# Double-buffered v, the first expert's arithmetic on GpSimd and wider slot rows in an attention and mixture-of-experts kernel

## The chip, the cores and the metric

The kernel runs on one core of a Trainium2 chip. The metric is the device time of one launch in microseconds. Three runs of the kernel before took 496.51, 497.23 and 498.8 us; their median is 497.23.

## What is computed

Causal attention over 4 batches of 12 heads (448 positions, 64 dimensions, float32), and then, on its output as 1792 rows of 768, a mixture of eight experts in which each row goes to its best expert only:

```python
scores = scale * np.matmul(q, k.transpose(0, 1, 3, 2))
scores = np.where(mask, -1000000000.0, scores)
attn = np.exp(scores - np.max(scores, axis=-1, keepdims=True))
attn = attn / (np.sum(attn, axis=-1, keepdims=True) + 1e-09)
x = np.matmul(attn, v)                       # 4 x 12 x 448 x 64, then rows of 768
...
logits = x @ w_gate + modality_bias[modality_id]
e_idx = np.argmax(logits, axis=1)
probs = softmax(logits)
out[mask] = gate_w[mask, None] * (np.maximum(x[mask] @ w1[e], 0.0) @ w2[e])   # for each expert e
```

## The kernel before

Float32 products are made from two parts: an operand is split into a high part (rounded to TensorE's fp32r) and a low part (the rest), and the product is three or four passes. The first three pairs of heads, the six that run before the split operands are ready, are multiplied in plain float32. Every split is one `tensor_scalar` (high) and one `tensor_tensor` (low) on some engine, and in attention most of them are GpSimd's.

**Attention** is a software pipeline. `iteration(n)`, n from 0 to 47 (the last heads' later stages follow behind), starts the scores of head n on TensorE (L270, `st_scores`), the exponentials of head n-1 on ScalarE (L290), the transposes (L302) and the split of the probabilities of head n-2 (L320 on ScalarE, L321 on VectorE), the product with v of head n-3 (L334, L341) and its output (L359, L365). Heads go in pairs m for q and k and in groups `gr` of four (`GH`) for v. For each pair GpSimd runs `split_qk` (L194, L195) and `split_kl` (L200 for the low part of k, L202 twice for q with one half zeroed, `qz`); SyncE stacks the parts with DMAs (L211, L212). For each group it runs `split_vh` (L242) and `split_vl` (L247) out of the one buffer `vraw`; those of group g + 1 stand at the end of iteration n = 4g + 2, and the next group's `load_v` (L235, L236), which must wait until they have read the buffer, at the start of n = 4g + 4.

A group's output is multiplied by wi, which holds both the identity and the gate's weights, and so gives rows of x and their partial logits. They are divided by the row sums in `norm_l` (L412) and `norm_x` (L422), on VectorE or, for the last of four row tiles, on GpSimd from a copy by ScalarE (L404). When a batch's last group is through (n = 19, 31, 43 for batches 0 to 2), `after_batch` puts its routing into the lists `later`, `before` and `soon`, which the iterations work off: logits (L454, VectorE), the best expert with ties broken (L457 to L470), slot numbers by a small chain of matmuls (`places`, L476 to L482) and a scatter of row numbers and gate weights into four tables in DRAM (L501, GpSimd's indirect DMA). Batch 3's routing runs after the pipeline. GpSimd also makes the constants (`setup_1`, `setup_4`, `shift_slots`, each a chain of instructions on a few elements) and splits w1 chunks 0, 1, 2, 3 and 5 of the first expert (L675, L676); from batch 1 the kernel already knows the expert with the most rows (`first_expert`, `first_slot`, `first_shift`, L516 to L537, VectorE).

**The end of attention** starts the first expert: `pre_g1(t, ks)` multiplies step t's rows by w1 chunks ks (L751 to L753). In the order of the code: pre_g1(0, 3 and 4), `places` of batch 3, pre_g1(1, 0 to 3), the ranks and batch 3's scatter, pre_g1(0, 5), relu, pre_g1(1, 4), the transposes of step 0, and so on. `ids_for(1)` then reads step 1's slots back from the tables, `fetch_x(1)` gathers its rows (L732, GpSimd) and L741 transposes them. From there to the end the experts' steps run on TensorE almost without a gap.

Every engine works its own queue in program order; so where an instruction stands in GpSimd's queue decides what must be done ahead of it. An entry of a table is 8 bytes; an expert has 1792 places of its own in a table, followed by an empty region, 14592 entries in all.

Of the kernel before, what the change touches and what calls it, by code (L numbers as in the profile page):

```python
# [21 lines left out]
def attention_moe(  # L22
# [23 lines left out]
    GH = 4  # L46
# [14 lines left out]
    NS = 32  # L61
    EMPTY = E * NT
    NROW = EMPTY + 2 * BLK
    BIG = 30000
# [10 lines left out]
    def sm(shape, tag, dt=F32, bufs=2):  # L75
        return small.tile(shape, dt, tag=tag, name=tag, bufs=bufs)
# [148 lines left out]
    def first_load(m):  # L225
        nc.sync.dma_start(out=first_view(m, 2), in_=qk[0, m, :, 1])
        for a in range(2):
            r = slice(a * 64, a * 64 + 64)
            (nc.sync if m or a else nc.scalar).dma_start(out=first_view(m, a)[r], in_=qk[0, m, r, 0])
            spl[2 * m + a] = (first_view(m, a), first_view(m, 2), None, None)  # L230

    def load_v(gr):
        b, u = divmod(gr, NG)
        c = slice(u * GH * D, (u + 1) * GH * D)
        nc.sync.dma_start(out=vraw[:, 0:3, :], in_=v[b, 0:384, c].rearrange("(t p) c -> p t c", p=128))  # L235
        nc.sync.dma_start(out=vraw[0:64, 3, :], in_=v[b, 384:448, c])  # L236

    vsrc = vraw.rearrange("p t (h d) -> p t h d", h=GH)

    def split_vh(gr):  # L240
        t = T([128, NTL, GH, 2, D], F32R, "vhl", 2)
        P.tensor_scalar(out=t[:, :, :, 0], in0=vsrc, scalar1=1.0, scalar2=0.0, op0=ALU.mult, op1=ALU.add)  # L242
# [198 lines left out]
    def route(b):  # L441
# [30 lines left out]
        def places():  # L472
            prev = rt[b - 1][0][:, NP:] if b else ebase
# [12 lines left out]
            A.activation(out=pe[:, :, 0:E], in_=lg, func=AF.Exp)  # L486
            rt[b] = (pc, si)
# [19 lines left out]
        if b == B - 2:  # L507
            choose = ((1, logits), (1, top), (1, ties), (2, first_tie), (-3, choice))
        return choose, places, (slots, ranks), scatter
# [4 lines left out]
    def counts(b):  # L514
        cnt = sm([128, E], "cnt")
        V.tensor_tensor(out=cnt, in0=rt[b][0][:, NP:], in1=ebase, op=ALU.subtract)  # L516
        return cnt
# [3 lines left out]
    def first_expert():  # L521
        cnt = counts(1)
        fe["m"] = m = sm([128, 1], "fm")
        fe["t"] = t = sm([128, E], "ft")
        V.tensor_reduce(out=m, in_=cnt, axis=AX, op=ALU.max)
        V.scalar_tensor_tensor(out=t, in0=cnt, scalar=m, in1=e8[:, 0, :], op0=ALU.is_ge, op1=ALU.mult)

    def first_slot():
        V.tensor_reduce(out=xf, in_=fe["t"], axis=AX, op=ALU.max)
        V.scalar_tensor_tensor(  # L530
            out=sch0[0:1, 0:1 + NPRE], in0=sch_a, scalar=xf[0:1], in1=sch_b, op0=ALU.mult, op1=ALU.add
        )
        V.tensor_scalar(out=oh0, in0=fe["t"], scalar1=xf, scalar2=None, op0=ALU.is_equal)

    def first_shift():
        V.tensor_scalar(out=shift, in0=fe["m"], scalar1=float(2 * BLK), scalar2=None, op0=ALU.is_lt)
        V.scalar_tensor_tensor(out=now, in0=by_shift[1], scalar=shift, in1=by_shift[0], op0=ALU.mult, op1=ALU.add)  # L537

# [29 lines left out]
    def schedule_a(cnt):  # L568
# [13 lines left out]
        def ts(o, a, x, y, op0, op1):  # L582
            V.tensor_scalar(out=o, in0=a, scalar1=x, scalar2=y, op0=op0, op1=op1)
# [41 lines left out]
        red(r, base)  # L625
        ts(sch[:, 0:1], r, float(EMPTY), 0.0, ALU.add, ALU.add)
        return seg, oh
# [81 lines left out]
    def fetch_ids(t, off, blk=0):  # L709
        d = early.tile([128, NTL, 2, 2], I32, tag="idq", name="idq", bufs=3)  # L710
        for i in range(NTL):
            o = d[:, i, blk]
            if t == 0 or PZ <= t < SZ:
                src = tables[i][bass.ds(off, BLK), :]
            elif t < PZ:
                o = d[:, i]
                src = tables[i][bass.ds(off, 2 * BLK), :].rearrange("(b p) c -> p b c", p=BLK)
            else:
                src = tables[i][bass.ds(off, HB), :].rearrange("(o p) c -> o p c", o=1).to_broadcast([2, HB, 2])
            nc.sync.dma_start(out=o, in_=src)  # L720
        idq[t, blk] = d
# [155 lines left out]
    with tc.manual_schedule():  # L877
# [51 lines left out]
        ti = it[:, 256:257]  # L929
        P.memset(onesf, 1.0)  # L930
        P.memset(eq, 0.5)
        P.memset(sch_a, -float(NT))
        P.memset(sch_a[:, 0:1], -1.0)
        for j in range(1 + NPRE):
            P.memset(sch_b[:, j:j + 1], float(E * NT + (j - 1) * BLK) if j else float(E))
        for j in range(2):
# [16 lines left out]
        def later(n, f):  # L953
            todo.setdefault(n, []).append(f)
# [30 lines left out]
        def setup_1():  # L985
            cmp(gpos, eq1, 0.0, ALU.is_gt)
            P.tensor_tensor(out=gt64, in0=gpos, in1=gt64, op=ALU.mult)
            cmp(eq1, eq1, -1.0, ALU.is_equal)
            cmp(ctri, ctri, 0.0, ALU.is_gt)
            fma(e8, evals, -1.0, float(E))  # L990
            P.tensor_copy(e8v, e8)
            fma(ebase, evals[:, 0, :], float(NT), 0.0)
            fma(ebneg, ebase, 1.0, -float(EMPTY))

        later(0, setup_0)
        later(1, setup_1)
        later(2, lambda: V.memset(e8v[64:128, 0], 0.0))

        def setup_4():
            P.iota(ent[:, :, 0, 0], pattern=[[S, B]], base=0, channel_multiplier=1)  # L1000
            P.iota(ent[:, :, 1:NTL, 0], pattern=[[S, B], [128, NTL - 1]], base=64, channel_multiplier=1)
            for i in range(NTL):
                nc.sync.dma_start(out=tables[i].rearrange("(p r) c -> p r c", p=128), in_=fill)
            it = row()
# [25 lines left out]
        def after_batch(b, n):  # L1030
# [4 lines left out]
            for j, f in choose:  # L1035
                later(n + j, f) if j > 0 else before(n - j, f)
            last = b == B - 2
            soon(n + 4, places)
# [35 lines left out]

        for k in range(KA):
            later(NHEAD - KA + k, lambda k=k: w1_chunk(k, P))
        later(4, setup_4)
        for s in range(2):
            for j in range(3):
                later(6 + 3 * s + j, lambda s=s, j=j: shift_slots(s, j))  # L1080

        def iteration(n):
            if n % 2 == 1 and 5 < n + 3 < NHEAD:
                stack_qk((n + 3) // 2)
            if n == 1:
                load_v(1)
            if n and n % GH == 0 and n // GH + 1 < B * NG:
                load_v(n // GH + 1)
            gr, i = divmod(n - 2 * GH, GH)
# [17 lines left out]
            if n == 0:  # L1107
                split_vh(0)
                split_vl(0)
            if n % 2 == 1 and 5 < n + 3 < NHEAD:  # L1110
# [18 lines left out]
            if 0 <= gr < B * NG:  # L1129
                st_comb(gr, i)  # L1130
            if n % GH == 2 and n // GH + 1 < B * NG:
                split_vh(n // GH + 1)
                split_vl(n // GH + 1)
            if n in (1, 3):
                load_qk(4 + n // 2)
            if n % 2 == 0 and n > 3 and n + 8 < NHEAD:
                load_qk((n + 8) // 2)

        for n in range(NHEAD):
# [99 lines left out]
        def w2_chunk(*ks):  # L1239
            split_w(raw20, w2h, w2l, ks)  # L1240
# [185 lines left out]
```

## Time and profile before

| | |
|---|---|
| median of three runs | 497.23 us (496.51 to 498.8) |
| the profiled execution | 498.88 us, its span 496.8 us |
| mean granted TensorE clock | 0.987 |
| TensorE busy (matmul) | 470.7 us, 95% |
| VectorE, ScalarE, GpSimd busy | 290.3, 276.4, 245.8 us |
| DMA | 78.91 MB, mean 159 GB/s |

The table is of one profiled execution; its own time stands beside its span because the span leaves out what lies around the first and last instruction. Shares are means over the span: attention fills about the first 210 us, the experts the rest, and GpSimd, VectorE and ScalarE are much busier in the first part.

### The profile page before, as it was taken

The numbers are of one execution on the slowest core, as the hardware profiler recorded it, in microseconds if no ns is written. First come the engines' busy times: TensorE is split into PE (matmuls) and PEld (weight loads), VectorE is DVE, ScalarE is ACT, GpSimd is POOL, SyncE is SP. The second block draws the span as 40 slices with busy tenths as digits, with TensorE's granted clock in tenths as the row PEclk, the third lists the DMA queues.
The fourth block names the chain that finished last, engine by engine and source line by source line (L and its number), as shares of the span: only waits on it lengthen the run. The fifth ranks groups of instructions, "written<-read, shape, count | busy, mean of one in ns | idle before, by whom it ended". The sixth has DMA issues, their size and how long they took to land. (4 is left out here: it accounts for less than half of the span.)

```text
span 496.8 us, 10248 instructions
## 1 busy us (share of the span) xinstructions
PE 470.7 (95%) x3307; PEld 443.0 (89%) x3307; DVE 290.3 (58%) x858; ACT 276.4 (56%) x680; POOL 245.8 (49%) x332
## 2 busy tenths in 40 slices
PE   8999899999899979989999999999999999999990
PEld 6799899999798979869999999999999999889770
DVE  4899899999889988987422017431120120283490
ACT  5799899999788978326212116612220211383670
POOL 8999999999999999942301104102001001021131
PEclk9999999999899999989999999999999999999997
DMA  7797799998987889491596204853001001076200
GB/s 189 199 257 214 183 236 251 281 237 206 292 214 182 188 182 327 126 202 3 163 381 208 81 1 144 292 203 98 34 1 53 33 2 63 33 279 194 104 13 7
DMA packets 43816, 78.91 MB, mean 159 GB/s; under 512 B 15582, under 2 KB 27614, under 8 KB 43744
## 3 DMA queue, kind: packets, MB, share of 16 engines
q1 hardware_dynamic: 40624, 66.94, 49.2%
q0 software_dynamic: 3040, 11.03, 6.6%
q8 instruction: 28, 0.46, 0.5%
q14 instruction: 44, 0.36, 0.3%
q10 hardware_dynamic: 80, 0.11, 0.1%
HBM read 48.10 MB, written 11.89 MB: 121 GB/s over the span
## 5 line engine op out<-in xcount | busy, mean ns | idle before, releaser
L732 POOL DMA_INDIRECT xg<-xs,idg x18 | 21.0, 1164 | 156.6 <-DVEq L1336 80.8
L290 ACT ACTIVATE p<-p,nm 128x448 f32<-128x448 f32 x192 | 94.8, 498 | 2.5 <-DVE nm L280 2.5
L770 DVE SCALAR_TENSOR_TENSOR htl<-g,hth 128x256 fp32r<-128x256 f32 x40 | 16.7, 425 | 104.6 <-ACT hth L769 104.6
L751 PE MATMUL g<-xh,w1h 128*128 128x256 f32 x240 | 67.1, 280 | 0.4 <-DVE htl L770 0.4
L753 PE MATMUL g<-xh,w1l 128*128 128x256 f32 x240 | 67.3, 280 | 0.0
L752 PE MATMUL g<-xl,w1h 128*128 128x256 f32 x240 | 67.0, 279 | 0.0
L321 DVE TENSOR_TENSOR pl<-pt,ph 128x1024 fp32r<-128x1024 f32 x48 | 58.3, 1215 | 7.6 <-ACT ph L320 7.2
L302 PE MATMUL pt<-ident,p 128*128 128x128 f32 x480 | 60.2, 273 | 0.0
L302 PEld LDWEIGHTS pt<-ident,p 128*128 128x128 f32 x480 | 55.3, 141 | 1.1
L334 PE MATMUL ot<-ph,vhl 128*128 128x448 f32 x192 | 50.5, 303 | 5.9 <-DVE ut L365 5.9
L320 ACT ACTIVATE ph<-pt 128x1024 fp32r<-128x1024 f32 x48 | 49.1, 1023 | 7.4 <-PE pt L302 6.3
L769 ACT ACTIVATE hth<-g 128x256 fp32r<-128x256 f32 x40 | 15.1, 383 | 63.5 <-PE g L753 63.5
L751 PEld LDWEIGHTS g<-xh,w1h 128*128 128x128 f32 x240 | 44.9, 187 | 0.6 <-DVE htl L770 0.6
L811 POOL DMA_INDIRECT out_dram<-row,idg x14 | 16.2, 1157 | 59.1 <-ACTq L1320 33.5
L752 PEld LDWEIGHTS g<-xl,w1h 128*128 128x128 f32 x240 | 45.2, 188 | 0.0
L753 PEld LDWEIGHTS g<-xh,w1l 128*128 128x128 f32 x240 | 45.1, 188 | 0.0
L334 PEld LDWEIGHTS ot<-ph,vhl 128*128 128x128 f32 x192 | 33.2, 192 | 7.9 <-DVE ut L365 6.4
L280 DVE CUSTOM_DVE_ANT_0 p<-sa,mask 128x448 f32<-128x448 f32 x96 | 36.2, 412 | 5.2 <-PE sa L270 4.9
L290 ACT ACTIVATION_READ_ACCUMULATOR p<-p,nm 128x1 f32 x192 | 36.5, 190 | 0.0
L280 DVE CUSTOM_DVE_ANT_0 p<-sb,mask 128x192 f32<-128x192 f32 x96 | 36.3, 411 | 0.0
L341 PE MATMUL ot<-pl,vhl 128*64 128x64 f32 x192 | 35.1, 298 | 0.7 <-DVE pl L321 0.7
L359 ACT ACTIVATE hol<-ot 64x448 f32<-64x448 f32 x48 | 26.0, 542 | 13.3 <-PE ot L334 10.8
(365 smaller groups left out, 1307.6 us busy)
## 6 DMA issues: line engine op xcount, KB each, us to landing
st<-hl SPq DMA_DIRECT2D x56, 224.0 KB
raw<-in_moe_w_dram SPq DMA_DIRECT2D x24, 512.0 KB
raw<-in_qk_dram SPq DMA_DIRECT2D x21, 448.0 KB
raw<-in_moe_w_dram SPq DMA_DIRECT2D x20, 384.0 KB
vraw<-in_v_dram SPq DMA_DIRECT2D x12, 384.0 KB
xs<-row SPq DMA_DIRECT2D x9, 384.0 KB
w1h<-hl SPq DMA_DIRECT2D x14, 224.0 KB
w1l<-hl SPq DMA_DIRECT2D x14, 224.0 KB
```

The source lines that it names most:

```text
L280: V.tensor_tensor_reduce(out=z, in0=o, in1=m, scale=-scale, scalar=3.0e38, op0=ALU.add, op1=ALU.min, accum_out=nm[:n, i:i + 1],)
L290: A.activation(out=z, in_=z, func=AF.Exp, bias=nm[:n, i:i + 1], scale=-1.0, accum_out=sums[:n, b, i, h:h + 1],)
L302: nc.tensor.transpose(out=o, in_=a, identity=i)
L320: A.activation(out=ph, in_=t, func=AF.Copy)
L321: V.tensor_tensor(out=pl, in0=t, in1=ph.bitcast(F32), op=ALU.subtract)
L334: nc.tensor.matmul(o[:, q0:S], lhsT=t[:rows, kt, h].rearrange("p a d -> p (a d)"), rhs=ph[:rows, c0:c1], start=(n == 0), stop=(n == 1),)
L341: nc.tensor.matmul(o[0:D, q0:S], lhsT=t[:rows, kt, h, 0], rhs=pl[:rows, c0:c1], start=False, stop=False)
L359: A.activation(out=t, in_=ov[g][64:128, :S], func=AF.Copy)
L732: P.indirect_dma_start(out=xg[u][:n], out_offset=None, in_=xs[0:rows, :], in_offset=bass.IndirectOffsetOnAxis(ap=g[:n, 0:1], axis=0), boun ...
L751: nc.tensor.matmul(o, lhsT=ah, rhs=bh, start=first, stop=False)
L752: nc.tensor.matmul(o, lhsT=ah, rhs=bl, start=False, stop=False)
L753: nc.tensor.matmul(o, lhsT=al, rhs=bh, start=False, stop=last)
```

## The change

The change has several parts. Places in the text of the kernel after the change have other line numbers (L412 becomes L421, L676 becomes L691, and so on).

- **v has two buffers**: `vraw`, and a raw w1 tile for even groups from 2 on. Loads go out earlier, at n = 1, 4 and then 4g + 2; `split_vh` moves from the end of n = 4g + 2 to that of 4g + 3, and so from ahead of the L412 of that iteration to behind it; `split_vl` goes to the end of n = 4g + 4. The very first `split_vl` goes from GpSimd to VectorE.
- **The first expert's arithmetic** goes from VectorE (six instructions, two reductions stay) to GpSimd (eleven).
- **The constants**: `setup_4` at n = 1 and not 4; the tables are cleared at n = 5; all of `shift_slots` at n = 3 and not over n = 6 to 11; one more constant.
- **Batch 2's choice** of expert stands ahead of the first w1 split.
- **Slot rows** are 64 bytes apart (every eighth 8-byte entry), the tables 20480 entries long; the slot numbers are multiplied by 8 where ScalarE copies them (L485 of the kernel before), and divided again for the counts.
- **The end**: pre_g1(0, 5) stands ahead of `places`; 32 warm-up matmuls in place of 24.

```diff
-    EMPTY = E * NT
-    NROW = EMPTY + 2 * BLK
+    STEP = 8
+    SHIFT = 64
+    EMPTY = STEP * (NT + E * SHIFT)
+    NROW = EMPTY + STEP * 2 * BLK
...
+    vraws = [vraw, raw1[2].rearrange("p (t c) -> p t c", t=NTL)]
+    def v_of(gr):
+        return vraws[gr > 1 and gr % 2 == 0]
...
-    def split_vl(gr):
+    def split_vl(gr, eng):
         t = vhl[gr]
-        P.tensor_tensor(out=t[:, :, :, 1], in0=vsrc, in1=t[:, :, :, 0].bitcast(F32), op=ALU.subtract)
+        eng.tensor_tensor(out=t[:, :, :, 1], in0=vsrc(gr), in1=t[:, :, :, 0].bitcast(F32), op=ALU.subtract)
...
-            A.activation(out=pc, in_=pos[:, 0:NP + E], func=AF.Copy)
+            A.activation(out=pc, in_=pos[:, 0:NP + E], func=AF.Copy, scale=float(STEP))
...
     def first_expert():
-        cnt = counts(1)
+        cnt = sm([128, E], "cnt")
+        ts(cnt, rt[1][0][:, NP:], 1.0 / STEP, 0.0)
+        P.tensor_tensor(out=cnt, in0=cnt, in1=ebase, op=ALU.subtract)
         V.tensor_reduce(out=m, in_=cnt, axis=AX, op=ALU.max)
-        V.scalar_tensor_tensor(out=t, in0=cnt, scalar=m, in1=e8[:, 0, :], op0=ALU.is_ge, op1=ALU.mult)
+        P.tensor_scalar(out=t, in0=cnt, scalar1=m, scalar2=0.0, op0=ALU.is_ge, op1=ALU.add)
+        P.tensor_tensor(out=t, in0=t, in1=e8[:, 0, :], op=ALU.mult)
...
     def first_slot():
         V.tensor_reduce(out=xf, in_=fe["t"], axis=AX, op=ALU.max)
-        V.scalar_tensor_tensor(
-            out=sch0[0:1, 0:1 + NPRE], in0=sch_a, scalar=xf[0:1], in1=sch_b, op0=ALU.mult, op1=ALU.add
-        )
-        V.tensor_scalar(out=oh0, in0=fe["t"], scalar1=xf, scalar2=None, op0=ALU.is_equal)
+        P.tensor_scalar(out=sch_a, in0=sch_a, scalar1=xf[0:1], scalar2=0.0, op0=ALU.mult, op1=ALU.add)
+        P.tensor_tensor(out=sch_a, in0=sch_a, in1=sch_b, op=ALU.add)
+        P.tensor_copy(sch0[0:1, 0:1 + NPRE], sch_a)
+        P.tensor_scalar(out=oh0, in0=fe["t"], scalar1=xf, scalar2=0.0, op0=ALU.is_equal, op1=ALU.add)
...
-                src = tables[i][bass.ds(off, BLK), :]
+                src = tables[i][bass.ds(off, BLK, STEP), :]
...
-        for _ in range(24):
+        for _ in range(32):
...
-            later(3 + j, lambda j=j: V.memset(xg[j], 0.0))
+            later(2 * j, lambda j=j: V.memset(xg[j], 0.0))
...
-        later(2, lambda: V.memset(e8v[64:128, 0], 0.0))
+        later(3, lambda: V.memset(e8v[64:128, 0], 0.0))
...
-        for k in range(KA):
-            later(NHEAD - KA + k, lambda k=k: w1_chunk(k, P))
-        later(4, setup_4)
+        later(1, setup_4)
+        later(5, clear_tables)
         for s in range(2):
             for j in range(3):
-                later(6 + 3 * s + j, lambda s=s, j=j: shift_slots(s, j))
+                later(3, lambda s=s, j=j: shift_slots(s, j))
...
-            if n % GH == 2 and n // GH + 1 < B * NG:
+            if n == 1:
+                split_vl(0, V)
+            if n == 2 or n % GH == 3 and n > GH and n // GH + 1 < B * NG:
                 split_vh(n // GH + 1)
-                split_vl(n // GH + 1)
+            if n == 2 or n % GH == 0 and n > GH:
+                split_vl((n + 2) // GH, P)
...
         pre_g1(0, (3, 4))
+        pre_g1(0, (5,))
         places()
         pre_g1(1, (0, 1, 2, 3))
...
-        pre_g1(0, (5,))
         ha, hb = (relu(o, i) for i, o in enumerate(g1b[0]))
-        w2_chunk(2)
         pre_g1(1, (4,))
         pa, pb = two_banks()
         h_trans(0, ha, 0, pa)
+        w2_chunk(2)
```

GpSimd's queue near the start, before the change: the split of pair 3 (heads 6 and 7) around the v split of group 1, then the first of setup_4's instructions (L1000 on).

```order
L194 TENSOR_SCALAR hl<-raw_121 128x896
L195 TENSOR_TENSOR hl<-raw_121,hl 128x448
L242 TENSOR_SCALAR vhl<-vraw 128x16x64
L247 TENSOR_TENSOR vhl<-vraw,vhl 128x16x64
L200 TENSOR_TENSOR xh<-raw_121,hl 128x448
L202 TENSOR_SCALAR w1h_147<-raw_121,half 128x448 x2
L1000 IOTA ent 128x4
L1001 IOTA ent 128x4x3
```

The same place after the change, from the second of the two slot tables' instructions on (those of the first, and setup_4, stand ahead of this piece; L202 and L204 are L200 and L202 of before):

```order
L559 TENSOR_SCALAR by_shift_99<-tcol 128x1 x2
L559 TENSOR_SCALAR by_shift_99<-by_shift_99 128x1 x2
L559 TENSOR_SCALAR slot<-by_shift_99 128x1
L571 TENSOR_SCALAR by_shift_99<-by_shift_99,slot 128x1
L559 TENSOR_SCALAR slot<-by_shift_99 128x1
L571 TENSOR_SCALAR by_shift_99<-by_shift_99,slot 128x1
L573 TENSOR_TENSOR by_shift_99<-by_shift_99,by_shift_98 128x4
L202 TENSOR_TENSOR xh<-raw_121,hl 128x448
L204 TENSOR_SCALAR w1h_147<-raw_121,half 128x448 x2
```

All 17 instructions of the slot tables and the eight of setup_4 now stand ahead of the last two splits of pair 3; before, they stood behind them.

GpSimd's queue where the first expert is found, iterations 37 and 38, after the change (`cnt`, `ft`, `sch_a` and `oh_95` are the counts, the candidates, the schedule's first row and the one-hot choice; `fm` and `xf` come from VectorE):

```order
L256 TENSOR_TENSOR vhl<-vraw,vhl 128x16x64
L559 TENSOR_SCALAR cnt<-pc 128x8
L537 TENSOR_TENSOR cnt<-cnt,ebase 128x8
L539 TENSOR_SCALAR ft<-cnt,fm 128x8
L540 TENSOR_TENSOR ft<-ft,e_80 128x8
L202 TENSOR_TENSOR xh<-raw_120,hl 128x448
L204 TENSOR_SCALAR qz_155<-raw_120,half 128x448 x2
L381 TENSOR_SCALAR rec<-sums 128x16
L544 TENSOR_SCALAR sch_a<-sch_a,xf 1x3
L545 TENSOR_TENSOR sch_a<-sch_a,sch_b 1x3
L546 CAST sch_110<-sch_a 1x3
L547 TENSOR_SCALAR oh_95<-ft,xf 128x8
```

Before, the splits and L381 (then L372) follow one another there with none of the eight small instructions between them.

TensorE's queue at the end of attention, after the change: the last chunk of step 0 and the first instruction of `places`.

```order
L766 MATMUL sa_3222<-w1h5_3215,xh_130 128x512
L767 MATMUL sa_3222<-w1l5_3216,xh_130 128x512
L768 MATMUL sa_3222<-w1h5_3215,xl_131 128x512
L766 MATMUL sb_3223<-w1h5_3215,xh_130 128x512
L767 MATMUL sb_3223<-w1l5_3216,xh_130 128x512
L768 MATMUL sb_3223<-w1h5_3215,xl_131 128x512
L485 MATMUL x_3406<-pc_2829,onesf_82 128x40
```

Before, chunk 4's matmuls stood right ahead of `places` (L476 then), and these six came only after the 24 of pre_g1(1, 0 to 3).

## Rows read from the trace of the kernel before

**Rows 1.** The profile page: busy time and instructions of each engine over the span.

```profile
PE 470.7 (95%) x3307; PEld 443.0 (89%) x3307; DVE 290.3 (58%) x858; ACT 276.4 (56%) x680; POOL 245.8 (49%) x332
```

**Rows 2.** GpSimd's waits, 8 to 216 us: line, releaser: total, times, longest.

```profile
POOL vhl L242 <- DMA vraw<-in_v_dram: 1.4, 1, 1.4
POOL xg L732 <- DVE m L465: 0.5, 1, 0.5
```

**Rows 3.** Windows table: stretch, length, busy PE, PEld, DVE, ACT, POOL, PEclk, DMA, GB/s.

```profile
9.76:209.18 199.42, 189.13 (x1478) 178.49 (x1477) 181.67 (x594) 174.84 (x494) 188.85 (x244) 0.99 0.86 222
```

**Rows 4.** Timeline of GpSimd, 10 to 28 us: start, length, line, operation.

```profile
10.89 2.36 POOL L247 TENSOR_TENSOR vhl<-vraw,vhl 128x1024 fp32r<-128x1024 f32 x1
...
22.56 1.26 POOL L202 TENSOR_SCALAR w1h<-raw,half 128x448 fp32r<-128x448 f32 x2
...
26.42 0.94 POOL L194 TENSOR_SCALAR hl<-raw 128x896 fp32r<-128x896 f32 x1
```

**Rows 5.** Timeline of GpSimd, 37 to 39 us: two of the slot rows' operations.

```profile
37.79 0.19 POOL L544 TENSOR_SCALAR slot<-by_shift 128x1 f32<-128x1 f32 x1
38.08 0.31 POOL L556 TENSOR_SCALAR by_shift<-by_shift,slot 128x1 f32<-128x1 f32 x1
```

**Rows 6.** Timeline of TensorE: the start, heads 6 and 14, and 132 us.

```profile
1.12 2.74 PE L892 MATMUL x<-ones 128*128 128x128 bf16 x24 [1.12 <-DVE warm L894]
...
25.61 0.37 PE L270 MATMUL sa<-xh,w1h 128*128 128x448 f32 x1
...
56.99 0.47 PE L270 MATMUL sa<-xl,qz 128*128 128x448 f32 x1 [1.60 <-POOL qz L202]
...
132.16 0.74 PE L334 MATMUL ot<-ph,vhl 128*128 128x448 f32 x2 [2.11 <-DVE ut L365]
```

**Rows 7.** Timeline of VectorE: the logits of batch 1.

```profile
129.18 0.93 DVE L454 TENSOR_REDUCE lg<-ltp 128x32 f32<-128x416 f32 x1 [1.58 <-POOL ltp L412]
```

**Rows 8.** Windows table again: TensorE's granted clock after three idle stretches.

```profile
56.99:60.00 3.01, 3.01 (x25) 2.96 (x26) 1.68 (x9) 1.16 (x3) 2.93 (x4) 1.00 0.46 133
132.20:135.40 3.20, 3.20 (x14) 3.07 (x15) 3.20 (x12) 1.19 (x4) 2.91 (x4) 0.53 1.05 381
214.30:217.60 3.30, 3.30 (x10) 2.56 (x9) 3.19 (x15) 0.59 (x1) 0.91 (x2) 0.50 1.20 173
```

**Rows 9.** Timelines of ScalarE and GpSimd: normalising the head group of n = 19.

```profile
75.50 0.41 ACT L404 ACTIVATE cxt<-x 128x288 f32<-128x288 f32 x1
...
81.69 0.25 POOL L412 TENSOR_TENSOR ltp<-cxt,rec 128x32 f32<-128x32 f32 x1
```

**Rows 10.** The page's groups: VectorE's split of the probabilities.

```profile
L321 DVE TENSOR_TENSOR pl<-pt,ph 128x1024 fp32r<-128x1024 f32 x48 | 58.3, 1215 | 7.6 <-ACT ph L320 7.2
```

**Rows 11.** Timelines of GpSimd and VectorE: the end of attention, 208 to 211 us.

```profile
208.23 0.95 POOL L412 TENSOR_TENSOR ltp<-cxt,rec 128x32 f32<-128x32 f32 x1
...
210.19 1.00 DVE L454 TENSOR_REDUCE lg<-ltp 128x32 f32<-128x416 f32 x1
```

**Rows 12.** Timeline of TensorE: batch 3's slot numbers, first expert's last chunk.

```profile
213.21 0.38 PE L476 MATMUL x<-pc,onesf 1*128 1x40 f32 x2 [1.61 <-DVE row L422]
...
220.89 0.40 PE L751 MATMUL sa<-w1h,xh 128*128 128x512 f32 x1
...
222.29 0.40 PE L751 MATMUL g<-w1h,xh 128*128 128x512 f32 x1
```

**Rows 13.** Timeline of GpSimd: batch 3's first scatter; landings of all sixteen scatters.

```profile
220.07 0.99 POOL L501 DMA_INDIRECT table<-ent,si  x1 [4.85 <-DVE i L580]
...
DMA to landing us min/median/max: 4.3/7.3/9.4
```

**Rows 14.** Step 1's gather on GpSimd, its landing, its transposes on TensorE.

```profile
236.20 1.02 POOL L732 DMA_INDIRECT xg<-xs,idg  x1 [0.30 <-PE sb L779]
...
DMA to landing us min/median/max: 3.9/3.9/3.9
...
241.19 0.27 PE L741 MATMUL g<-ident,xg 128*128 128x128 f32 x1
```

More of the change, by code (lines that the diff above doesn't have):

```diff
@@ L234, in load_v, with vsrc @@
         c = slice(u * GH * D, (u + 1) * GH * D)
[L235 to L238 removed]
+        t = v_of(gr)
+        nc.sync.dma_start(out=t[:, 0:3, :], in_=v[b, 0:384, c].rearrange("(t p) c -> p t c", p=128))
+        nc.sync.dma_start(out=t[0:64, 3, :], in_=v[b, 384:448, c])
+    def vsrc(gr):
+        return v_of(gr).rearrange("p t (h d) -> p t h d", h=GH)
     def split_vh(gr):
         t = T([128, NTL, GH, 2, D], F32R, "vhl", 2)
[L242 removed]
+        P.tensor_scalar(out=t[:, :, :, 0], in0=vsrc(gr), scalar1=1.0, scalar2=0.0, op0=ALU.mult, op1=ALU.add)
         vhl[gr] = t
[L245 removed]
+    def split_vl(gr, eng):
         t = vhl[gr]
[L247 removed]
+        eng.tensor_tensor(out=t[:, :, :, 1], in0=vsrc(gr), in1=t[:, :, :, 0].bitcast(F32), op=ALU.subtract)
     SPOS = [(0, 448), (1, 0), (1, 192), (0, 0)]
@@ L472, in places @@
         def places():
-            prev = rt[b - 1][0][:, NP:] if b else ebase
+            prev = rt[b - 1][0][:, NP:] if b else fe["eb"]
             ohf = oh.rearrange("p t e -> p (t e)")
@@ L507, in route @@
         if b == B - 2:
-            choose = ((1, logits), (1, top), (1, ties), (2, first_tie), (-3, choice))
+            choose = ((1, logits), (1, top), (1, ties), (2, first_tie), (2, choice))
         return choose, places, (slots, ranks), scatter
@@ L515, in counts @@
         cnt = sm([128, E], "cnt")
-        V.tensor_tensor(out=cnt, in0=rt[b][0][:, NP:], in1=ebase, op=ALU.subtract)
+        V.scalar_tensor_tensor(
+            out=cnt, in0=rt[b][0][:, NP:], scalar=1.0 / STEP, in1=ebase, op0=ALU.mult, op1=ALU.subtract
+        )
         return cnt
@@ L713, in fetch_ids @@
             if t == 0 or PZ <= t < SZ:
-                src = tables[i][bass.ds(off, BLK), :]
+                src = tables[i][bass.ds(off, BLK, STEP), :]
             elif t < PZ:
                 o = d[:, i]
-                src = tables[i][bass.ds(off, 2 * BLK), :].rearrange("(b p) c -> p b c", p=BLK)
+                src = tables[i][bass.ds(off, 2 * BLK, STEP), :].rearrange("(b p) c -> p b c", p=BLK)
             else:
-                src = tables[i][bass.ds(off, HB), :].rearrange("(o p) c -> o p c", o=1).to_broadcast([2, HB, 2])
+                src = tables[i][bass.ds(off, HB, STEP), :].rearrange("(o p) c -> o p c", o=1).to_broadcast([2, HB, 2])
             nc.sync.dma_start(out=o, in_=src)
@@ L929, in attention_moe @@
         ti = it[:, 256:257]
-        P.memset(onesf, 1.0)
+        P.memset(onesf, 1.0 / STEP)
         P.memset(eq, 0.5)
-        P.memset(sch_a, -float(NT))
+        P.memset(sch_a, -float(STEP * SHIFT + 1))
         P.memset(sch_a[:, 0:1], -1.0)
         for j in range(1 + NPRE):
-            P.memset(sch_b[:, j:j + 1], float(E * NT + (j - 1) * BLK) if j else float(E))
+            P.memset(sch_b[:, j:j + 1], float(E * (STEP * SHIFT + 1) + (j - 1) * BLK * STEP) if j else float(E))
         for j in range(2):
@@ L991, in setup_1 @@
             P.tensor_copy(e8v, e8)
-            fma(ebase, evals[:, 0, :], float(NT), 0.0)
-            fma(ebneg, ebase, 1.0, -float(EMPTY))
+            fma(ebase, evals[:, 0, :], SHIFT + 1.0 / STEP, 0.0)
+            fma(ebneg, ebase, 1.0, -float(EMPTY // STEP))
+            fe["eb"] = sm([128, E], "cnt")
+            fma(fe["eb"], ebase, float(STEP), 0.0)
         later(0, setup_0)
         later(1, setup_1)
-        later(2, lambda: V.memset(e8v[64:128, 0], 0.0))
+        later(3, lambda: V.memset(e8v[64:128, 0], 0.0))
         def setup_4():
@@ L1001, in setup_4 @@
             P.iota(ent[:, :, 1:NTL, 0], pattern=[[S, B], [128, NTL - 1]], base=64, channel_multiplier=1)
-            for i in range(NTL):
-                nc.sync.dma_start(out=tables[i].rearrange("(p r) c -> p r c", p=128), in_=fill)
             it = row()
@@ L1036, in after_batch @@
                 later(n + j, f) if j > 0 else before(n - j, f)
-            last = b == B - 2
+            if b == B - 2:
+                before(n + 3, lambda: w1_chunk(0, P))
+                before(n + 4, lambda: w1_chunk(1, P))
+                later(n + 4, lambda: w1_chunk(2, P))
             soon(n + 4, places)
@@ L1073, in open_psm, with clear_tables @@
             mo["ps"] = ctx.enter_context(tc.tile_pool(name="psm", bufs=4, space=PSUM, reuse_waits="tile"))
-        for k in range(KA):
-            later(NHEAD - KA + k, lambda k=k: w1_chunk(k, P))
-        later(4, setup_4)
+        def clear_tables():
+            for i in range(NTL):
+                nc.sync.dma_start(out=tables[i].rearrange("(p r) c -> p r c", p=128), in_=fill)
+        later(1, setup_4)
+        later(5, clear_tables)
         for s in range(2):
             for j in range(3):
-                later(6 + 3 * s + j, lambda s=s, j=j: shift_slots(s, j))
+                later(3, lambda s=s, j=j: shift_slots(s, j))
         def iteration(n):
@@ L1084, in iteration @@
                 stack_qk((n + 3) // 2)
[L1085 to L1088, printed above, removed]
             gr, i = divmod(n - 2 * GH, GH)
@@ L1137, in iteration @@
                 load_qk((n + 8) // 2)
+            if n in (1, 4):
+                load_v(n // GH + 1)
+            if n % GH == 2 and n > GH and n // GH + 2 < B * NG:
+                load_v(n // GH + 2)
         for n in range(NHEAD):
```

10 lines of the change are left out of this document (6 added, 4 removed).

## The prediction

> **What bounds the kernel now.** The page's busy line comes first [rows 1]: TensorE works 95% of the span, GpSimd 49%. That half is an average over two stages, so the second view is GpSimd's list of waits over the attention stage [rows 2]. It holds hardly anything: 1.4 us for the first v tile and half a microsecond at a gather are its longest. The windows table says the same of the whole stretch from 9.76 us to the end of GpSimd's last normalisation [rows 3]: 188.85 of 199.42 us busy in 244 instructions, the rest being pauses of under a tenth of a microsecond between instructions. TensorE is busy 189.13 us there. **In attention GpSimd's queue is one unbroken list**, and its length sets when the last logits can be normalised. TensorE's own stalls, the ones that the change goes for, are mostly pauses until GpSimd catches up.
>
> The timeline shows three such places. At head 14 TensorE waits 1.60 us for GpSimd's qz [rows 6]. At 129 us VectorE's logits of batch 1 wait 1.58 us for GpSimd's norm [rows 7], ahead of which stand in the queue the 3.4 us of a v split (1.05 and 2.36), and TensorE then waits 2.11 us [rows 6]; after that its granted clock is 0.53, the 1.2 GHz level, for 3.2 us [rows 8], which costs 3.2 x 0.47 = 1.5 us. At the end it stands 1.61 us before batch 3's slot numbers [rows 12], and the next 3.3 us run at 0.50 [rows 8], so half of them, 1.6 us, is lost. The wait at head 14 cost no clock [rows 8].
>
> **The change part by part.** I count on GpSimd's list first, up to the end of its last L412 at 208.23 + 0.95 = 209.18 us [rows 11].
> The first v_lo split goes to VectorE: -2.4 [rows 4]. One more constant: +0.3, at the 0.29 us spacing of dependent small instructions [rows 5]. The first expert's arithmetic: VectorE loses six instructions, GpSimd gains eleven in chains, 11 x 0.29 = +3.2. VectorE keeps the two reductions between them, so GpSimd waits twice for it; each wait is from nothing to one split that VectorE is in the middle of, 1.2 us [rows 10]. VectorE runs ahead of GpSimd (in rows 7 it waits for it), so it will stand ready and I take 0.15 each, +0.3 (0 to 2.4). Its first reduction then waits for GpSimd's counts, and behind it on VectorE stand a split and L365, for which TensorE waits; that pause, like the others, ends where GpSimd's list lets it, and is not added. The wait of 0.5 us at the gather [rows 2] goes, since a v split now stands ahead of it. The two halves of the other v splits only change places: 0 on the list. The w1 splits and the third choice too: the same instructions in another order.
>
> The setup moves cost nothing in sum but much at one place. Setup_4 (26.42 less the end of L202 at 22.56 + 1.26 = 23.82, so 2.6 us [rows 4]) and all 17 slot-row instructions now stand ahead of the third pair's kl and qz. A dependent pair takes 2 x 0.29, a lone one 0.19 [rows 5], so the seventeen take 3.2 to 4.9 us; 4.1 is the middle. Its qz ends at 23.82 - 2.4 + 0.3 + 2.6 + 4.1 = 28.4, the first half of it 0.6 earlier, and TensorE wants that half at 25.61 [rows 6]: **a new stall of 2.2 us at head 6**. That is nearest to the 2.11 us idle that lost the clock, but the 1.60 kept it and the 1.61 lost it, so 0 or 1.5 us more. Eight more warm-up matmuls (24 take 2.74 us [rows 6], so 0.9) lie at the start, where that stall swallows them.
>
> That late TensorE then makes GpSimd wait, which it never did. The norm at n = 19 has its copy ready at 75.91 and gets to it at 81.69 [rows 9], 5.8 us of reserve, of which 3.4 goes because the v split no longer stands in front of it: 2.4 left. TensorE is later by 2.2 (or 3.7), less the 1.6 us of head 14 that it need no longer wait; GpSimd is 2.1 earlier by then. The gap closes by 2.7 or 4.2, so GpSimd waits 0.3 or 1.8 us; I take the middle, +1.1.
>
> Sum on the list: -2.4 + 0.3 + 3.2 + 0.3 - 0.5 + 1.1 = +2.0 us. Batch 3's logits start 1.0 us after the list's end, at 210.19, held by VectorE's own queue [rows 11], so they come **1.0 us later**. The stalls removed at 57 and 132 us are not in this sum: TensorE gets through earlier and waits for later entries of the same list.
>
> Then the gain. The first expert's last w1 chunk is six matmuls, 222.29 - 220.89 = 1.4 us [rows 12], that now run in the idle time ahead of the slot numbers: **-1.4**. That idle is then 1.61 + 1.0 - 1.4 = 1.2 us, less than the 1.60 that kept the clock, so the 1.6 us at half speed go as well: -1.6. TensorE would reach step 1's transposes at 241.19 + 1.0 - 1.4 - 1.6 = 239.2. But their gather lands at 236.20 + 3.9 = 240.1 [rows 14], 1.0 later after the change: 241.1, and nearly all is waited away, -0.1. Unless the scatters land sooner: step 1's ids are read back from the tables, and batch 3's first scatter is issued after 4.85 us of idle [rows 13] that its DVE releaser does not fill, so I put it down to batch 2's entries still being on the way. Rows 64 bytes apart may shorten the landings, which lie between 4.3 and 9.4 us with rows of one spacing [rows 13]; 1.9 us sooner in all gives TensorE its whole 2.0. Bounds: 0 and 5.1 us per scatter. I take the middle of the effect: -0.1 and -2.0 make **-1.1**.
>
> The Trainium skill, "DMA: Bandwidth & Descriptors", section Specifications, has transfers below 512 bytes done by read-modify-write. The entries stay 8 bytes, so by that rule the spacing buys nothing and the sum is -0.1. No row here shows a scatter at another spacing.
>
> The other edits lie under this: ScalarE's scale costs nothing in an instruction that is there anyway; the table fill is 0.4 times larger but issued by SyncE long before the first scatter; the xg and e8v memsets are VectorE's, in its gaps.
>
> **The sum.** The profiled execution took 498.88, its span 496.8. 498.88 - 1.1 = 497.8. The median of the runs, 497.23, is 1.65 lower, so I forecast **496.1 us**. With GpSimd's waits at their low ends the logits come on time and all 3.0 us is kept, 494.2; with the 1.8 us wait the logits are 1.7 late, the idle is 1.9, the clock falls as now, and it ends at +0.3, 497.6. So 494.2 to 497.6 for this case. Half a percent, 2.5 us, is about what a measurement here can tell from no change.
>
> **The rivals.**
> *The list gets shorter (faster).* GpSimd's last L412 took 0.95 us where the same instruction took 0.25 at n = 19 [rows 9, 11], beside VectorE's work. If the moves of work from VectorE end such overlaps (-0.7), if the clock survives head 6 and the copy at n = 19 is ready, the list is -2.4 + 0.3 + 3.2 - 0.5 - 0.7 = -0.1; VectorE, no longer behind TensorE's stalls, follows the list, so the logits come up to 1.1 early; with 1.4, 1.6 and scatters that land soon that is -4.1: 493.1 us. For it: rows 7's wait is the queue's order alone and is truly gone. Against it: eleven added instructions.
> The Trainium skill, "GPSIMD Engine Reference", section Specifications, says that GpSimd shares its SBUF interfaces with VectorE's two-input instructions. The 0.95 against 0.25 agrees with it, and by it this rival would be the likelier.
>
> *GpSimd hands back and forth with VectorE (slower).* At head 37 and 38 GpSimd stands each time until VectorE's reduction is through, behind a 1.2 us split [rows 10]: 2.4 us, and the clock is lost at head 6, so 1.8 at n = 19. The list is -2.4 + 0.3 + 3.2 + 2.4 - 0.5 + 1.8 = +4.8; the logits come 3.8 later, the clock falls as before, and with 1.4 back that is +2.4: 499.6 us. It decides from 1.0 + 1.4 = 2.4 us on the list upward. For it: the list has no slack at all [rows 3]. Against it: VectorE is ahead of GpSimd at that place.
>
> *The spacing does nothing.* The landings stay as they are and step 1's transposes wait for their rows whatever TensorE saved: -0.1, 497.1 us. For it: the entries are as small as ever. Of the change's named parts "six plain heads" is no edit at all: both kernels have them.
>
> **How the numbers follow.** Forecast 0.46, shorter list 0.29, hand-backs 0.16, idle spacing 0.09. The shorter list is faster by over 2.5 us nine times in ten, the forecast case one time in eight: 0.26 + 0.06 = 0.32. Slower by over 2.5 us is the upper half of the hand-backs, 0.10, and 0.04 of the head 6 stall growing, 0.14. The rest, 0.54, is within. The range runs from half a microsecond under the first rival to just under the second: 492.6 to 499.4.
>
> **What would show it.** Right: GpSimd again without gaps up to 209 to 212 us; a TensorE wait of 2 us or more at head 6 for qz; no wait of batch 1's logits; the six matmuls ahead of L485 and a granted clock near full behind it; scatters landing earlier than 7.3 us in the median. Wrong: GpSimd's list ending before 208 or after 213, no stall at head 6, or step 1's transposes waiting for the gather by more than a microsecond.

## The result, and the profile after

The changed kernel is **slower**: 504.6 us in the median of four runs (503.9 to 505.08), the kernel before 497.86 beside it (496.51 to 498.8, four runs); ratio 1.0117, interval 1.0081 to 1.0153. The forecast was 496.1 with a range up to 499.4, so both the sign and the range were wrong. The profiled execution took 505.08 us, its span 503.2.

The page's busy line and the granted clock by slices of the span, after the change:

```profile
PE 471.9 (94%) x3315; PEld 443.7 (88%) x3315; DVE 292.4 (58%) x854; ACT 276.1 (55%) x680; POOL 249.3 (50%) x343
PEclk9998999999999999989999999999999999999996
```

Against [rows 1] TensorE has eight small matmuls more in a longer span, and GpSimd 3.5 us more work. The larger part of the time was lost to waits: GpSimd's list of waits over the attention stage (line, releaser: total, times, longest) shows some that [rows 2] did not have:

```profile
POOL ltp L421 <- ACT cxt L413: 4.1, 3, 2.1
POOL hl L196 <- DMA st<-hl: 2.9, 1, 2.9
...
POOL eq L478 <- DVE m L474: 1.0, 1, 1.0
...
POOL ft L539 <- DVE fm L538: 0.3, 1, 0.3
```

4.1 us are for ScalarE's copies at three norms (2.05 at 53 us, 1.04 at 68 us, 1.04 at 83 us, which is the norm of n = 19), 2.9 us for stacks of q and k that SyncE's DMAs had not yet read out of `hl`, and 1.0 for VectorE at a choice of expert (L478). The feared hand-back with VectorE, L539 for fm, is 0.3 us. The timelines of the end of attention (GpSimd's last norm, VectorE's logits, TensorE's slot numbers, the transposes of step 1) answer to [rows 11, 12, 14]:

```profile
215.91 0.95 POOL L421 TENSOR_TENSOR ltp<-cxt,rec 128x32 f32<-128x32 f32 x1
...
217.87 1.02 DVE L463 TENSOR_REDUCE lg<-ltp 128x32 f32<-128x416 f32 x1
...
220.94 0.38 PE L485 MATMUL x<-pc,onesf 1*128 1x40 f32 x2 [2.00 <-DVE row L431]
...
247.47 0.82 PE L756 MATMUL g<-ident,xg 128*128 128x128 f32 x6
```

GpSimd's last norm starts at 215.91 and not at 208.23: **7.7 us later, where the sum had +2.0**. Everything behind follows it. The slot numbers stand 5.0 us behind the norm in both kernels. Step 1's transposes stand 31.6 us behind it and not 33.0: those 1.4 us are what the six matmuls were priced at.

### The profile page after: what moved, and what is told of

Same layout as the page of the kernel before. It is cut to its first block, busy times and chain, and to the rows that moved or that the text cites. A ratio compares the mean times of both kernels' runs of the same rounds, so it can differ in the third digit from the quotient of the medians.

```text
span 503.2 us, 10272 instructions
## 1 busy us (share of the span) xinstructions
PE 471.9 (94%) x3315; PEld 443.7 (88%) x3315; DVE 292.4 (58%) x854; ACT 276.1 (55%) x680; POOL 249.3 (50%) x343
## 5 line engine op out<-in xcount | busy, mean ns | idle before, releaser
L826 POOL DMA_INDIRECT out_dram<-row,idg x14 | 19.6, 1398 | 59.2 <-ACTq L1345 33.5
```

## The experiments

"End" in the table is the start of GpSimd's last norm in each profiled execution: 208.23 in the kernel before, 215.91 in the changed one. Names with a_ are edits of the changed kernel, those with b_ of the kernel before. The medians of the kernel before, measured beside them, lie between 497.45 and 498.16.

| run | what it is | median us | ratio to before, interval | end |
|---|---|---|---|---|
| a_consts | constants back | 497.39 | 1.0002 (0.9985 to 1.0019) | 208.71 |
| a_first | first expert back on VectorE | 500.91 | 1.0058 (1.0033 to 1.0083) | 212.69 |
| a_both | both | 494.75 | 0.9941 (0.9919 to 0.9963) | 209.42 |
| b_slots | slot rows at 3 | 498.44 | 1.0017 (0.9998 to 1.0036) | 207.97 |
| a_slots | slot rows back only | 498.99 | 1.0040 (1.0010 to 1.0070) | 209.93 |
| a_clears | clearing at 9 | 500.24 | 1.0070 (1.0040 to 1.0100) | 210.73 |
| b_consts | all constants moved | 502.99 | 1.0090 (1.0061 to 1.0119) | 212.68 |
| b_consts9 | the same, clearing at 9 | 499.82 | 1.0046 (1.0029 to 1.0062) | 209.68 |
| b_rows_g1 | spaced rows, six matmuls early | 497.14 | 0.9984 (0.9971 to 0.9996) | 207.85 |
| b_v | v's two buffers | 495.44 | 0.9960 (0.9943 to 0.9978) | 205.52 |
| b_first | first expert on GpSimd | 501.51 | 1.0082 (1.0051 to 1.0113) | 211.43 |
| a_load | v load ahead of a blocked load | 503.66 | 1.0119 (1.0077 to 1.0160) | 215.34 |
| a_both_rows1 | a_both, rows 8 bytes apart | 494.54 | 0.9938 (0.9917 to 0.9958) | 206.32 |
| best1 | a_both, two splits later | 491.77 | 0.9880 (0.9856 to 0.9903) | 202.13 |

The profiled execution of a_both was the slowest of its runs (497.58), so its end is late for its median.

### The two costly parts

```diff
-        later(1, setup_4)
-        later(5, clear_tables)
+        later(4, setup_4)
+        later(4, clear_tables)
...
-                later(3, lambda s=s, j=j: shift_slots(s, j))
+                later(6 + 3 * s + j, lambda s=s, j=j: shift_slots(s, j))
```

> The changed kernel with setup_4, the clearing of the tables and the slot-row constants back at iterations 4 and 6 to 11. Stuck loads (theory A): the constants ahead of the third pair's last splits hold a load that stands first in SyncE's queue, the DMA engines fall idle from 24 to 30 us, and the three early TensorE waits (2.55, 1.09 and 3.54 us) and most of GpSimd's new waits (2.90 for stacks, 2.05 + 1.04 + 1.04 for ScalarE's copies) come of it: all of them go, and the time falls by 4 to 6 us, to 498.5 to 500.5. Longer list (theory B): only the eleven added GpSimd instructions and their hand-backs matter, the early stall is waited for later anyway: at most 1 us less, 503.5 to 505.

It fell by 7.2 us to 497.39, more than theory A allowed, and its end is the 7.2 us earlier too. None of GpSimd's waits for copies or stacks is left. a_first takes the functions `first_expert`, `first_slot` and `first_shift` from the kernel before.

> The changed kernel with the first expert's arithmetic back on VectorE (eleven GpSimd instructions fewer). Theory A: GpSimd's list is shorter by the 11 x 0.29 = 3.2 us and the 0.3 us wait for fm, so 3 to 3.5 us less, 501 to 501.7, with the early stalls as they are. Theory B: nearly the whole difference to the kernel before goes, 5 to 6 us less, 498.5 to 499.5. If neither the list nor the hand-backs set the end: no change, 504.6.

> Both of the above undone together; v's two buffers, the spaced slot rows, batch 2's choice and the end phase's order stay as changed. Theory A: the two add up, 8 to 9 us less than the change: 495.5 to 497, one to two below the kernel before. Theory B: 498.5 to 499.5, as with the arithmetic alone. If v's two buffers or the other order themselves cost something, it stays at or above the 497.9 of the kernel before.

a_first is 3.7 us faster than the change, by the arithmetic alone. Both together give 494.75, 9.9 less than the change, a little under the sum, and below the kernel before: theory A holds in the main, theory B falls. b_first puts the same functions into the kernel before:

> The kernel before with the first expert's arithmetic on GpSimd alone: eleven instructions more there, six fewer on VectorE. If GpSimd's unbroken list sets the end of attention, its length counts fully: 3 to 4 us slower, 500.5 to 501.5. If VectorE's slowed instructions at 150 us (0.51 and 0.89 us) are worth moving away: 497 or less.

It is 3.4 us slower. The timelines of GpSimd's last norm and of TensorE's slot numbers in it show where:

```profile
211.43 0.96 POOL L412 TENSOR_TENSOR ltp<-cxt,rec 128x32 f32<-128x32 f32 x1
...
216.41 0.38 PE L476 MATMUL x<-pc,onesf 1*128 1x40 f32 x2 [1.56 <-DVE row L422]
```

Both are 3.2 us later than in [rows 11, 12], which is eleven instructions at 0.29 us; the one wait for VectorE in between (L528 for fm) is 0.3 us, and VectorE's lighter queue has gained nothing that shows. GpSimd's list sets the end of attention here, and what is added to it counts fully.

### Why the constants cost so much

> The kernel before with one edit: all seventeen slot-row instructions at iteration 3, ahead of the third pair's last splits. Theory A: their 4.1 us delay the split, TensorE waits at head 6 (up to 4 us, since this kernel's setup_4 stays behind), SyncE's next load waits as long; 1 to 4 us slower, 499 to 502. Theory B: the instructions are the same number on the list, so no change, 497.4 to 498.4.

Only 1.0 us, an interval that holds no change, though TensorE waited twice (total, times, longest):

```profile
PE sa L270 <- POOL w1h L202: 1.4, 1, 1.4
PE sa L270 <- DMA st<-hl: 1.6, 1, 1.6
```

So three microseconds of TensorE's stall were taken up by GpSimd's reserve, the kind that the prediction counted on: GpSimd shows no wait for a copy or a stack in this run, and the end is not later at all.

> The kernel before with all the moves of constants: setup_4 at 1, the clearing at 5, the slot rows at 3; v keeps one buffer and its splits stand ahead of the norms. If the early TensorE stall costs by itself: 5 to 7 us slower, 502.5 to 504.5. If GpSimd's reserve against ScalarE's copies (5.8 to 6.8 us in the kernel before) takes the stall, and it costs only because the new v order used 3.4 us of that reserve: 0 to 2 us slower, 497.4 to 499.5, and GpSimd shows no wait for ScalarE's copies.

5.4 us slower, so my second idea, that the stall costs only where the new v order has used up the reserve, fell. Here is what TensorE waits for in it, and the windows behind (columns as in [rows 3]):

```profile
29.52 0.74 PE L270 MATMUL sa<-xh,w1h 128*128 128x448 f32 x1 [4.35 <-POOL w1h L202]
...
55.88 0.44 PE L270 MATMUL sa<-w1h 128*128 128x448 f32 x1 [2.60 <-DMA w1h<-hl]
```

```profile
28.00:30.00 2.00, 0.48 (x1) 0.48 (x2) 0.00 (x0) 0.00 (x0) 2.00 (x3) 0.50 0.00 0
30.00:36.00 6.00, 6.00 (x35) 5.82 (x35) 2.80 (x10) 2.04 (x4) 5.66 (x9) 0.65 0.72 206
```

The wait at head 6 is 4.35 us in this kernel, and the clock is 0.50 and 0.65 for the 8 us after. Then pair 6's stack comes 2.60 us late. GpSimd waited 1.9 us for v buffers, 1.7 for stacks, 0.5 for a copy, and 2.0 and 1.7 for VectorE.

The next two take the one and the other cause out of the changed kernel:

```diff
-                later(3, lambda s=s, j=j: shift_slots(s, j))
+                later(6 + 3 * s + j, lambda s=s, j=j: shift_slots(s, j))
```

> The changed kernel with only the slot-row constants back at iterations 6 to 11; setup_4 stays at 1 and the clearing of the tables at 5. Undoing all constants gave 7.2 us. If the delay of the third pair's split is what matters (4.1 of its 6.7 us go, so SyncE's blocked load and the empty DMA engines nearly go too): 4 to 7 us less than the change, 497.5 to 500.5. If the clearing of the tables in SyncE's queue between two stacks is what matters: at most 2 us less, 502.5 to 504.6.

```diff
-        later(5, clear_tables)
+        later(9, clear_tables)
```

> The changed kernel with only the clearing of the tables later, at iteration 9 and not 5. If it is the clearing (2.5 us of SyncE's queue and 640 KB ahead of pair 5's stacks) that makes the 3.54 us wait at head 10: 3 to 5 us less, 499.5 to 501.5. If it is the delayed split and the DMA time lost before: under 1 us, 503.6 to 504.6.

a_slots is 5.6 and a_clears 4.4 us faster than the change, together more than the 7.2 of both: each is enough to bring most of it back. It is the two at once that cost. (The ten runs of each spread over 6 us, 497.16 to 503.05 and 498.66 to 505.1, so the difference between the two says little.) In a_clears the DMA engines still move nothing from 26 to 28 us and TensorE still waits 3.06 us at head 6, but no later wait in the first 64 us reaches over 1.0. How much the clearing makes in the kernel before:

> The kernel before with setup_4 at 1 and the slot rows at 3 as in the change, but the tables cleared at iteration 9; with the clearing at 5 this kernel cost 5.4 us. If the delayed split alone makes that (TensorE's 4.35 us wait and the half clock behind it): 502.5 to 503.5 still. If, as in the changed kernel, the clearing in front of pair 5's stacks makes over half of it: 499.5 to 501.

1.9 us slower in place of 5.4, so the clearing makes over half there as well. The wait at head 6 is 4.37 us in it, as long as in b_consts. **So the stall at head 6 alone is the smaller part of the cost; most comes when the clearing adds waits behind it.** TensorE's waits of over a microsecond in the first 64 us add up to 7.2 us in the changed kernel and 7.0 in b_consts, which cost 7.2 and 5.4 us; to 3.1 in a_clears, 3.7 in a_slots, 3.0 in b_slots and 4.4 in b_consts9, which cost 2.9, 1.6, 1.0 and 1.9 (a_ against a_consts, b_ against the kernel before). A reserve that takes the first of these waits and not the rest fits all six, but no run changes the reserve alone. The changed kernel's own trace shows how the waits arise. Those of over a microsecond:

```profile
28.01 0.47 PE L279 MATMUL sa<-xh,w1h 128*128 128x448 f32 x1 [2.55 <-POOL w1h L204]
...
36.12 0.44 PE L279 MATMUL sa<-st 128*128 128x448 f32 x1 [1.09 <-DMA st<-hl]
...
47.21 0.44 PE L279 MATMUL sa<-st 128*128 128x448 f32 x1 [3.54 <-DMA st<-hl]
```

The first is the stall that was forecast, 2.55 for 2.2. The others are for the stacks of pairs 4 and 5, and they were not. SyncE's queue (start, length, DMA, count; a length holds the waits within a group):

```profile
20.54 8.39 SPq L191 DMA_DIRECT2D raw<-in_qk_dram  x2
28.98 0.43 SPq L243 DMA_DIRECT2D raw<-in_v_dram  x1
...
30.05 0.54 SPq L213 DMA_DIRECT2D st<-hl  x1
...
33.74 2.52 SPq L1095 DMA_DIRECT2D table<-row  x4
...
37.91 0.54 SPq L213 DMA_DIRECT2D st<-hl  x1
```

The loads of q and k at 20.54 take 8.39 us because the second may not write its buffer before the third pair's last split, the one that now stands behind the constants; in SyncE's list of waits it is the longest of this group, 7.2 us:

```profile
SPq L191 <- POOL w1h L204: 9.9, 3, 7.2
```

Then come v, the stacks of pair 4, and at 33.74 the four clearings for 2.52 us, ahead of a load of q and k, one of v and, at 37.91, pair 5's stacks. In the windows the columns after the length are PE, PEld, DVE, ACT, POOL, clock, DMA share, GB/s:

```profile
22.00:24.00 2.00, 2.00 (x17) 1.79 (x16) 1.86 (x4) 1.92 (x8) 1.60 (x9) 1.00 0.98 243
...
26.00:28.00 2.00, 0.00 (x0) 0.00 (x0) 1.11 (x2) 1.86 (x8) 1.96 (x4) 1.00 0.00 0
...
42.00:45.00 3.00, 1.67 (x14) 1.42 (x12) 3.00 (x11) 2.88 (x9) 3.00 (x3) 1.00 1.06 208
48.00:50.00 2.00, 2.00 (x11) 1.96 (x10) 1.55 (x8) 0.00 (x0) 0.83 (x1) 0.50 1.06 195
222.00:224.00 2.00, 2.00 (x6) 1.52 (x6) 1.98 (x8) 1.60 (x3) 0.94 (x3) 0.50 0.97 253
```

From 26 to 28 us the DMA engines move nothing, with a share of 0.98 from 22 to 24, and from 30 us on they are full (1.06 from 42 to 45). The loads that were held back come now, together with the 640 KB of the clearing, and TensorE has pair 5's stacks only at 47.2. TensorE's clock is at 0.50 behind that wait.

One test went at the empty DMA engines alone, by letting the v load pass the blocked one:

```diff
+            if n == 4:
+                load_v(2)
             if n % 2 == 0 and n > 3 and n + 8 < NHEAD:
                 load_qk((n + 8) // 2)
-            if n in (1, 4):
-                load_v(n // GH + 1)
+            if n == 1:
+                load_v(1)
```

> The changed kernel with one pair of loads exchanged: at iteration 4 the v load stands ahead of the load of q and k that waits for the third pair's buffer. If SyncE's blocked queue matters by the DMA time that it wastes (none moved from 26 to 28 us): the v tile (448 KB, about 1.8 us at the 245 GB/s of the stretch before) comes in that time, and pair 5's stacks about that much earlier: 1 to 3 us faster than the change, 501.6 to 503.6. If the wait of TensorE at head 6 alone matters: no change, 504 to 505.

0.9 us less than the change, within the spread of both and short of the 1 to 3 that were expected. The edit did fill the gap in part: the DMA share from 24 to 26 us is 0.85 in place of 0.17, and TensorE's 1.09 us for pair 4 are gone. But pair 5's stacks are still issued at 37.88, behind the clearing, and TensorE still waits 3.56 us for them. So the idle DMA time is a small part; the clearing ahead of these stacks, with full DMA engines behind it, is the larger. How much of the 3.5 us is the order in the queue and how much the transfer of the 640 KB stays open: no run clears the tables with smaller or slower DMAs.

### The parts that were to gain

> The kernel before with two parts of the change only: the spaced slot rows and the six matmuls of step 0's last chunk ahead of batch 3's slot numbers. If these two carry the gain that is seen once the two costly parts are undone (-2.7): 494.3 to 495.5. If v's two buffers and the other order carry a part of it: 495.8 to 497, and the kernel with those (494.75) stays ahead. If the early gather only lets TensorE wait elsewhere: no change, 497.4.

It is 0.4 us faster. The slot numbers now follow the matmuls with 0.26 us of idle, but TensorE then waits at step 0's second product, for VectorE's part of h, which it did not before:

```profile
212.83 0.38 PE L478 MATMUL x<-pc,onesf 1*128 1x40 f32 x2 [0.26 <-DVE row L424]
...
224.81 0.44 PE L757 MATMUL ot<-w2h,htl 128*128 128x384 f32 x1 [1.61 <-DVE htl L786]
```

Of the gain of 1.4 to 3 us, 1.61 comes back as this wait. VectorE works off the schedule of batch 3 and w2's splits in the meantime. What became of the rest of that gain is not shown. The rows' spacing alone, taken out of a_both (`STEP = 1`, `SHIFT = NT`):

> The changed kernel with both costly parts undone and the slot rows 8 bytes apart again (scatters then land in 4 to 9 us and not in 2 to 5). If step 1's gather, which comes at the end of that chain, is what TensorE reaches first: 1 to 2 us slower than 494.75, 495.8 to 496.8. If TensorE gets to its transposes later than the rows either way: no change, 494.3 to 495.2.

494.54 against 494.75: the spacing changes nothing in the time. It does change the landings. Of all sixteen scatters, least, median and most, first in a_both, then with the rows 8 bytes apart:

```profile
DMA to landing us min/median/max: 2.1/3.8/5.2
```

```profile
DMA to landing us min/median/max: 3.5/5.8/7.7
```

The prediction's reading of the pause ahead of batch 3's first scatter fits: 4.85 us before, 4.42 in a_both_rows1, 1.00 in a_both. But the scatters do not set the time of step 1. VectorE waits 0.5 us for the slots read back in a_both_rows1 and not in a_both, and TensorE waits for step 1's rows in neither.

> The kernel before with v's two buffers and the new places of its splits alone (the first low split on VectorE). The kernel with both costly parts undone is 2.4 us faster than the one with rows and matmul order alone, so if v's buffers and order carry that: 494.5 to 496, with GpSimd's logits norm no longer waited for at 129 us. If that difference belongs to batch 2's choice and the w1 order: 497 to 498. GpSimd's list is 2.4 us shorter either way.

2.7 us faster. GpSimd's last norm comes 2.7 us earlier:

```profile
205.52 0.97 POOL L419 TENSOR_TENSOR ltp<-cxt,rec 128x32 f32<-128x32 f32 x1
```

That is close to the one 2.36 us split [rows 4] that VectorE has taken over, and no wait of the logits is left at batch 1. How large a share the second buffer has, apart from that split, was not tried.

### A faster version

```diff
-        w1_chunk(5, P)
         st_pv(n - 2)
...
         st_norm(g - 1, 3)
+        w1_chunk(5, P)
...
-        w2_chunk(0)
         st_sums(g, V)
...
         for _, f in choose:
             f()
+        w2_chunk(0)
```

> The changed kernel with both costly parts undone, and two splits moved at the end of attention: GpSimd splits w1 chunk 5 behind the last norm and not ahead of it, and VectorE's first w2 split stands behind batch 3's choice. GpSimd's norm then comes 3.4 us earlier, VectorE's logits (211.38 us in the kernel without this) about 2 us earlier, and the slot numbers can follow the six matmuls at once: the 1.49 us idle goes, 493 to 494 against its 494.75. If the later w1 or w2 parts are then waited for instead: 494.5 to 496.

491.77 us, 1.2% below the kernel before and 3.0 us below a_both, more than was expected. GpSimd's last norm, VectorE's logits and TensorE's slot numbers:

```profile
202.13 0.23 POOL L421 TENSOR_TENSOR ltp<-cxt,rec 128x32 f32<-128x32 f32 x1
...
204.95 1.04 DVE L463 TENSOR_REDUCE lg<-ltp 128x32 f32<-128x416 f32 x1
...
208.93 0.38 PE L485 MATMUL x<-pc,onesf 1*128 1x40 f32 x2 [0.49 <-DVE row L431]
```

The norm no longer stands behind 3.4 us of w1 split, the logits no longer behind a w2 split, and TensorE waits 0.49 us. The norm itself takes 0.23 us and not 0.96, with VectorE's w2 split gone from beside it. How the 3.0 us divide between the two moves was not tried.

## Why the prediction was wrong

- **What bounds attention: right.** GpSimd's list sets the end of attention. b_first and b_v move its end by +3.2 and -2.7 us and the time by +3.4 and -2.7.
- **The eleven instructions: right**, +3.2 in b_first for 3.2 and a hand-back of 0.3. The first split on VectorE: -2.7 for -2.4, with the second buffer.
- **The stall at head 6: right in place and nearly in size**, 2.55 us for 2.2. "The setup moves cost nothing in sum but much at one place" was right as well, but what follows from that place was priced too low.
- **The step that failed** is the price of the setup moves behind head 6: +1.1 us for GpSimd's wait at one norm, and nothing for "the table fill is 0.4 times larger but issued by SyncE long before the first scatter". That looked at who reads the tables and not at what stands behind the clearing in SyncE's queue. The runs show 4.1 us of waits for copies (1.04 of them at n = 19, where the 1.1 was put) and 2.9 for stacks. With 7.0 in place of 1.1 the sum of +2.0 becomes +7.9, and 7.7 were measured. Without the early clearing the constants cost 1.9 us in the kernel before, with it 5.4; in the changed kernel 2.9 and 7.2. The clearing costs this only on top of the delayed split: with the slot rows back and the clearing left, 1.6 us remain (a_slots). A number for it was in sight: [rows 3] has a mean DMA share of 0.86 over the whole stage, and the prediction did not use it.
- **Where the gain went.** The 1.4 us of the six matmuls were there. The idle ahead of the slot numbers was forecast at 1.2 us, as 1.61 plus the list's delay less 1.4, and is 2.00; 1.4 us of matmuls did not shorten it. It is 1.99 in a_consts too, where the norm is only 0.5 us later than in the kernel before, because TensorE is through with six more matmuls at 211.7 us, as early as it was without them. That TensorE would also come earlier is missing from the forecast of the idle. In b_rows_g1, where the idle was 0.26, the gain became a wait for VectorE.
- **The clock.** The forecast took the length of the idle stretch to decide, 1.60 or less keeping the clock and 1.61 losing it. The runs do not bear that out. The row 222 to 224 us above has 0.50 behind 2.00 us; a_consts keeps full clock behind 1.99 (its slot numbers, and the granted clock of its page by slices):

```profile
213.73 0.38 PE L485 MATMUL x<-pc,onesf 1*128 1x40 f32 x2 [1.99 <-DVE row L431]
PEclk9999999999999999999999999999999999999997
```

  So the 1.6 us that were to come back were read from one execution, and a shorter idle does not secure them.
- **The spacing** was worth -1.0 us in the sum, the middle of 0 and -2.0, and was worth nothing (494.75 against 494.54), though the landings came down from 5.8 to 3.8 us in the median. The term rested on step 1's transposes waiting for their gather. With the rows 8 bytes apart the gather stands 26.5 us behind GpSimd's last norm in place of the 28.0 of the kernel before: it came forward without the spacing. So the rival in which the spacing does nothing was right about the time, and wrong in that the landings stay and the transposes wait. The Trainium skill's rule on transfers below 512 bytes ("DMA: Bandwidth & Descriptors", Specifications) was read as "the spacing buys nothing"; the landings of the same 8-byte entries contradict that reading, and the time does not.
- **The rival that was slower** had the right sign, at 499.6, by the wrong mechanism: the hand-backs it was built on took 0.3 us of the 2.4 that it gave them.

## What to carry to other kernels

When an edit moves a DMA, price it by what is queued behind it on its issuing engine and by how full the DMA engines are there, not by when its own data is needed. When an engine's queue has no waits, its length is the time: add up what an edit puts on it, and take long work off the stretch ahead of its last dependent instruction. A stall with reserve behind it can be nearly free (b_slots); further waits on top of it are not (b_consts).

## What the runs showed of the hardware

- With the same entries of 8 bytes, scatters to rows 64 bytes apart landed after 3.5 us in the median in the changed kernel, 3.8 in a_both, 4.2 in a_consts and 4.2 in b_rows_g1; to rows 8 bytes apart after 7.3 in the kernel before [rows 13], 6.4 in b_v and 5.8 in a_both_rows1. The ranges overlap (2.1 to 7.7 in b_rows_g1, 3.5 to 7.7 in a_both_rows1).
- The length of an idle stretch of TensorE does not by itself tell whether the granted clock falls. It stayed full behind 1.58 us in b_v, 1.99 in a_consts, 2.55 at head 6 of the changed kernel and 3.06 at head 6 of a_clears. It fell to 0.50, the 1.2 GHz level, behind 1.56 in b_first and in b_slots, 2.00 at the slot numbers of the changed kernel and 3.54 at its head 10.
- GpSimd's norm of 128x32 took 0.23 us in best1 and 0.96 in a_both, where VectorE's w2 split ran beside it; that split took 2.91 us there, and 0.95 later in the same run.
